# A written order of 2718 commands: the first nine feed-forward pieces, their weight loads and casts stand earlier, and the first 1902 commands and the masks are another fit

## The chip, the cores and the metric

The kernel runs on one core of one Trainium2 chip. A core has TensorE (PE: matrix products, with its weight loads shown apart as PEld), VectorE (DVE), ScalarE (ACT), GpSimd (POOL) and SyncE (SP, which here issues nearly all DMAs). Each engine works through its own queue in the order in which the program was written and waits at an instruction until its operands are there. Products land in PSUM, everything else lives in SBUF.

The metric is the device time of one execution in microseconds, and the median of several. The profile describes one execution more closely; its span runs from the first to the last instruction.

## The reference

Two stages. First an attention with 8 batches, 8 heads, 576 positions and 64 dimensions a head, in which only scores within `tau` = 0.02 of the row's maximum count:

```python
scores = scale * np.matmul(q, k.transpose(0, 1, 3, 2))
thresh = np.max(scores, axis=-1, keepdims=True) - tau
scores = np.where(scores >= thresh, scores, -1000000000.0)
scores = scores - np.max(scores, axis=-1, keepdims=True)
attn = np.exp(scores)
attn = attn / (np.sum(attn, axis=-1, keepdims=True) + 1e-09)
return np.matmul(attn, v).astype(np.float32)
```

Its output, with the heads side by side, is x of 4608 x 512, and a feed-forward stage with three first matrices of 512 x 768 follows:

```python
h = np.maximum(np.maximum(x @ w1, x @ w2), x @ w3)
return (h @ w_out).astype(np.float32)
```

Inputs and output are float32.

## The kernel before

**Tiles.** The eight heads of a batch are handled as two quads of four heads, so there are 16 quads, numbered `g`. A quad's queries are cut into nine chunks; a chunk has 128 rows, two halves `r`, and one half tile is 128 x 576 scores. There are 16 x 9 x 2 = 288 half tiles. The first and the last batch (`SPLIT`) are worked in two parts: part 1 has chunks 0, 1, 5 and 6 of both quads (columns 0 to 255 of x), part 2 the other five (320 columns). So 16 half tiles come before the products of part 1 of batch 0, and 20 more before those of part 2.

**The order written out by hand.** All that comes after a short beginning (`beginning()`: the first transposes and two score tiles) is one text, `ORDER`, of 2718 commands; a command is one letter, and the letters S, T, O, F and D are followed by the number of the PSUM slot (0 to 3, two banks each) in which the result is put. `issue(what, where)` carries them out one after the other. Each letter takes the next item of its own list, so the text says when something is issued and not which. Every engine wrapper (`_Ordered`, line 92 holds its call, which is why all instructions of the profile bear L92) ties each instruction to the one before it on the same engine: the written order is the order in every queue. Here commands are counted from 0. The letters, by engine:

- TensorE: `S` the scores of a half tile (`sc`, two or four fp32 products); `T` the transposition of a quad's q or k (`tp`); `O` and `N` the products of probabilities and v (`o`); `D` spreads the first two quads' row scales (`d`); `F` the first eight matmuls of a feed-forward piece, `B` the other eight (both `ph`, or `po` where the piece is one of the output product).
- VectorE: `m` a half tile's maximum (a pass over 576 columns that accumulates); `k` the numerators of a half tile whose bit in `MASKED` is 1; `r`, `R` reciprocals; `c` copies k out of PSUM; `w` copies a product; `v` the maximum of a feed-forward product with what there is (`hm`, at the third matrix into `hT`).
- ScalarE: `e` the first pass over a half tile (an exponential with a 1 bit, else a leaky ramp `Prelu`); `n` the second pass, an exponential, for a half tile whose bit is 0; `a` copies q out of PSUM; `b`, `x`, `u` copies out of PSUM; `h` the copy of the first matrix's feed-forward product (`hm`).
- GpSimd: `p` scales a half tile's numerators to bf16 (`P`, from quad 2 on); `q` makes the copy of q with the halves of the partitions swapped (`qs`); `y` casts v; `z` casts one staged weight block of 128 x 1024 to bf16.
- SP: `l` one load of a quad's q, k or v; `g` one weight load of 512 KB into a `stage` buffer, of which there are two; `t` the DMA transposition of a chunk's `P` into `ptq`; `o` a store of 128 rows of the output.

**The masks.** A half tile's numerators are 0 for scores under the threshold. Two ways give the same values: with the bit at 1, `m` on VectorE writes -score to SBUF, `e` on ScalarE is the exponential and `k` on VectorE compares and multiplies; with the bit at 0, `m` keeps only the maximum, `e` is the ramp and `n` on ScalarE the exponential. `MASKED` holds 288 bits, one for each half tile in the order of the steps, and so shares the work between VectorE and ScalarE.

**Feed-forward pieces.** Nine pieces make a part's hidden rows in batch 0: three blocks of two times 128 hidden columns, times three matrices. Each has 16 matmuls of 64 rows by 256 columns (320 in part 2, 288 in later batches), an `h` or `v` step for it, and needs the block of weights that the `z` of the same number has cast, from the `g` of the same number. The first nine `g` and `z` are those of w1, w2, w3, the last three those of w_out. Part 1's pieces also need the four products `O` of part 1, which stand at commands 154 to 200 in this kernel, with their copies `w` until 207.

The lines that bear on it:

```python
elif what == "F":
    p = next(todo["F"])
    p.first(where)
    if p.second:
        pending.append(p)
elif what == "B":
    p = pending.pop(0)
    p.second()
    line[p.kind].extend(p.done)
elif what in "gz":
    next(loads if what == "g" else casts)()
```

Of the kernel before, what the change touches and what calls it, by code (L numbers as in the profile page):

```python
# [21 lines left out]
FLAT = 2.0 ** -100  # L22

MASKED = """
001011001000011010101101101000010111100001101000010100001010000100001000
001010100111100001001001000100110000011100010011001010001010010000111000
110010100101010010011100000001001011000110100110111001000100001110000101
001010001101110001100001000100100100001100001101010110110101000111111111
"""

# [8 lines left out]
PLACE = (0, 1, 4, 5, 6, 2, 3, 7, 8)  # L39

ORDER = """
mS2S3lmS1meenemelllgkllT0S2aqmlmeS3lmgT1lllT0eqckT2ancS0mtqS1qmennktyS3eteS2mznmS1eeS0mnlS3eS2S1mmS3netmegke
S2mS0mmyeS3znnRytyltleeS1nmkkeS0mmeeS2mS1enS0T3kmmktgltlemS1D2aS0eT3blekmmteS2D0O1ckmlO3bNwRwS0mneeD1knS3beT
2nD1tllabS0mS2ketnO1lRktmetmO3qNqtwqwzenT2nS0S1zncS3qymmS2mmeeS1S3D0S2mkmtD1elbeemneS0kmbkT3S1kegmatS2qS3neT
0memknneS2O1O3cNtS0remkwtqerT2pnaRmpS1D0gekrS2bmtlwneS0S3D1mmpplleblppzO2eO1mrqpNnekpS0wwS2nnmzF3S1S0emrmrmk
glBepqpF1pF2ethgzBevT3nBF0S1nncBvhS3S2pmrmgF0ekeT1BatnmrF3vS1BS0peF2rmpypS1lpBnvmezF3nhzBS2mpenekqvS1F0F3mtm
BqerkrBpgvepptT2cS1T0hnamttS3mnrS2tF0myBeS1ppeS2yvnplF3rS0nmemteeBlF1meqptS2pvT3BcmnF0tlS3znkphgglBemS1rvmS2
O3npemO0rknrNeewpF1xpS2qpS0ltntmF3lmneeBBS2S0rvhmF1tntpzleS3mBpF0S2empztvenrpBmpvS1mnS3S2enF0emrpS3pktS1pnme
rmmepBekuS2mkunenrS1S3pF0T2pmmtaBeueukpS1rpqeklmeS2tO3mprO0ekNS1lltlwlS2xmF3nF0BmepT1kBehrcF2nT3T1BvcppS0tlq
aqnllvF3qlmS1mrBprF2S0nekheBnmpvtF3S1BF2eS0mvtprmBypnpS1ehpytpS3mtoS2oeelmtmS0F3lF1meBkevryBT2yenF0vapT3cBT2  # L50
S1lS3naqhpF2qS0rkmBpmmrF3npeS1vempteneBvF2S0ktpmltrllBF3S1lnhnmBqrvpneelS0S2mpmO1ekreO3NT0xS2wcmS3mnpqpnF1F0
pBekpBvS2ertlS3F1htmtltmS0pBnemepynrF3eS2vS0mmrT1atppqeBS2pnpF1vF3meultkS0klT1enormkT2BaS2peS0ortcmnmuurS1pe
T2qpF3cS2mpenenpS0kmetrBmltS1S2puymlueeqpS0pylomO3mO1knNerekxwS0pmS2F3S1npnqmBF2elS0kmtBerkheF3pS1nmeypvBtrm
noF2leS0vpBS3rrmnpmpphS1ppF0etmS2emllBeF1nF3BtevkrpS0BvS2nS1hmmtleS3lmmetF2tkF0eBpleT1BvrvanT3nF2cS1BnmF0S3B
rhkF2mpeT1vnrBpprveaS0S3nmT1S2pqpncmpS0meeeqmeS1tO3pqmtotlloeO2ltqNF0S1klwBxrpkppS3mrhmF2S0epBmF3nenS1pvBF0m
F2nleBBtottvkS3hF0keF1rurvpmT2BeapkppyrpvS1S3mnS2S0pnemF1mtS2emkS3rpBenepltS0memkmrutpuS3neS2emF1rmpqkynpS3p
qeBemS0uuS3O2kmemekO1NeS0rwT3xoF1olppnT2mnT0BcS3aS2rncqhF0qtF1pBtemmpBkevrF3eS2vlmpnBptnlS0S1S2hermmempS3F0y
pmF1BBelrteoevnF2T3F0akkqvBBS3nhkymF1pqpnF2verBBS0rvtpmhnS3S1F2mrmlpBpeS0evlmS3eF1pnS2BmnleF3mtllvrlttS0eppp
tyBmS1ehF2lepT3BmltnS0lnltcS1rkvO3O2tmNpmeprT1nnexrapkwS0pqF2qyemT1T3cpBF0S1anepkBS3hvF2S0mreBF1mekmrnvF3qBe
S2vS0unpS3tS1omlrmeppqptlmmnF2pktT0BpecS1eekryuT3uaS0mnS2lomtmrtleF3enpS1kpS2qppnemmS0BmkerppeueqS1S0mnurO2k  # L60
mO1NkwxT0S3eeS1cmpmF2F0kkeBBhF3eF2pvrBS1nnBvpttS0hmemS3mrppF1rpS2BeenmeF0S3vBF1nkvmS2mlnBS0otolhF3llterlmF1k
BlpypvpBtvteeprS2F0rT3BpS1nnrmpmaS3mtpheS0S2emnF3eT1T0amecBS2ttoS0evyymmS1ppeO3mpqneO2NenqxF0kktF1wBT3lolrlk
lBpS2vphS0cmnF1mtlteS3nqrtBmrpF0vrpqpF2lekBeBpnhF1S3vmT0tlpBS2lS3avmpF0tF1mBrnelekS2evutppmrS3qppS1nS0nmF2mr
mS1peekenpS3BemmeS0rkS1emuS3tlT0ueT2mcknrannpepF1S0mS2qppBmtotlmlttkrrpeueS0qqmS2lO3ueemoeO0opptpkklNwS1lS2x
F3mS0BnemehF1kT2mrcnpBS0F3rvS2BltlpnmF1nepmeveS0pkmBS3httnF2eF1mBrBekF0nS3vrBprvpypppS2nmhemeS1S0F2pF3mmBeBr
T1eS0kvnapS2vF1nS3mnBrmmreS2F0pheS1meeBqpnS3mvmeypS1tpS2etlO0qO3mNpmT2neytF1xtlkkrtnweS3ppT0cramBF2S0Bnehvpp
meS1rF3qqmT2BF0ncveT2ktnBF3vS1mrnarBhppS0lF2T3qppeBmcS0S1ovmF3mneT2naepBvS0S2enF3mkmrkqpqueenF1nS3tmS0T2cpqB
eupurrS2mmottoS3pS0mttneelotpmS1O2mkkO0rNwrpeexpneF3nkpS0S2S1mBemS0euuppmF1erkS2tltlBptmrF3S0lhtpmeyppBeS1mv
O0O2NenmxpS3S1kF0mxemrS2kBF1enF3vBermF0tBhpyppyektBvS1pmF2F3vBkS1BF0nmehS2vrBmtpO3eotpnevO1NkF0S2krmnrpxpxBh
F3S1eBF0mS2F1BnvpmBrS3vS2S0ehemmF1kppmnF3rBvkBF2F0BF1ehBtkvevoF2pptkttO3O0NuprBwS2xS0vmmpeS3ekF1S2pmF0oeBmrB  # L70
okettF3peuokoruoF2uhF1pkkF3hvvruF2pF1F3hppF0pvvF2F1vvF3F0F2hvtovhtF1F3F0F2htvF1voF3O0uvO2NvF1xwF3hF2F0vF3vhF
2F0F3hvF2vvF0F3F2vF0hF3hovF2vF0F3vhF2vvF0vBuuF3BuouoF2uooo
"""


# [731 lines left out]
```

## Time and profile before

| | |
|---|---|
| median of 3 runs | 441.56 us (440.37 to 443.75) |
| the profiled execution | 439.98 us |
| its span | 438.2 us |
| TensorE busy | 420.6 us |
| VectorE busy | 398.2 us |
| ScalarE busy | 387.0 us |
| GpSimd busy | 288.5 us |
| TensorE's granted clock, mean | 1.00 |
| DMA | 87.45 MB, 200 GB/s |

Rows of the profile name an instruction by line, engine, operation and by what it writes and reads (`z<-sc,nm` writes z from sc and nm), then give its shape, the count, the summed busy time and the mean duration in ns of one, and after the second bar the engine's idle time just before them with what ended it. The rows of slices are the span in 40 equal parts of 11 us, each digit the busy share in tenths. Matmuls overlap, so the busy time of TensorE is the time in which at least one was under way, and the ends of matmuls are modelled.

### The profile page before, as it was taken

The numbers are of one execution on the slowest core, as the hardware profiler recorded it, in microseconds if no ns is written. First come the engines' busy times: TensorE is split into PE (matmuls) and PEld (weight loads), VectorE is DVE, ScalarE is ACT, GpSimd is POOL, SyncE is SP. The second block draws the span as 40 slices with busy tenths as digits, with TensorE's granted clock in tenths as the row PEclk, the third lists the DMA queues.
The fourth block names the chain that finished last, engine by engine and source line by source line (L and its number), as shares of the span: only waits on it lengthen the run. The fifth ranks groups of instructions, "written<-read, shape, count | busy, mean of one in ns | idle before, by whom it ended". The sixth has DMA issues, their size and how long they took to land.

```text
span 438.2 us, 14262 instructions
## 1 busy us (share of the span) xinstructions
PE 420.6 (96%) x5313; PEld 306.9 (70%) x5313; DVE 398.2 (91%) x1105; ACT 387.0 (88%) x784; POOL 288.5 (66%) x370
## 2 busy tenths in 40 slices
PE   7679889999999999999999999999999999999995
PEld 5446458776787767867787767877677776777762
DVE  3999999989999999999999999999999999999641
ACT  5999999999999999988999999989999999875422
POOL 3704288978688697596867885678759677554500
PEclk9999999999999999999999999999999999999999
DMA  7999999999999999999899998979989997485602
GB/s 252 302 241 206 221 229 261 237 244 193 211 192 225 229 200 193 205 174 256 185 203 216 222 190 206 212 201 219 201 220 186 246 150 154 110 160 128 177 14 109
DMA packets 212773, 87.45 MB, mean 200 GB/s; under 512 B 185824, under 2 KB 199648, under 8 KB 212704
## 3 DMA queue, kind: packets, MB, share of 16 engines
q1 hardware_dynamic: 212000, 85.69, 92.4%
q8 instruction: 42, 0.69, 0.7%
q10 hardware_dynamic: 704, 0.85, 0.6%
q14 instruction: 27, 0.22, 0.2%
HBM read 34.60 MB, written 9.44 MB: 101 GB/s over the span
## 4 chain that ended last, share of the span: by engine, by line
PE 81%; ACT 9%; DMA 3%; issue 2%; DVE 2%; POOL 2%; SPq 0%; POOLq 0%; DVEq 0%
PE ph L92 30%; PE sc L92 27%; PE po L92 11%; PE o L92 9%; ACT z L92 5%; PE tp L92 3%; DMA ptq<-P 3%; ACT P L92 2%; POOL P L92 1%; DVE z L92 1%; PE warm L92 1%; DVE unused L92 1%; ACT qt L92 1%; DMA out_dram<-ob 1%; PE d L92 0%
## 5 line engine op out<-in xcount | busy, mean ns | idle before, releaser
L92 POOL TENSOR_SCALAR P<-z,rs 128x576 bf16<-128x576 f32 x252 | 206.8, 833 | 78.9 <-DVE rs L92 27.4
L92 PE MATMUL sc<-kt,qt 64*128 64x256 f32 (+2 forms) x640 | 177.1, 421 | 2.7 <-DVE z L92 1.3
L92 PE MATMUL sc<-kt,qs 64*128 64x320 f32 (+2 forms) x640 | 175.5, 410 | 4.0 <-ACT z L92 1.6
L92 PE MATMUL ph<-xt,w 64*128 64x288 bf16 (+4 forms) x2160 | 170.5, 283 | 0.4 <-ACT z L92 0.2
L92 PEld LDWEIGHTS <-w 64*128 64x128 bf16 (+1 forms) x2160 | 124.4, 94 | 33.6 <-issue 6.3
L92 DVE TENSOR_SCALAR_CACHE_REDUCE unused<-sc 128x576 bf16<-128x576 f32 x170 | 124.8, 749 | 4.0 <-PE sc L92 3.2
L92 ACT ACTIVATE z<-sc,nm 128x576 f32<-128x576 f32 x170 | 122.7, 740 | 3.4 <-DVE unused L92 1.6
L92 PEld LDWEIGHTS sc<-kt,qs 64*128 64x128 f32 (+1 forms) x640 | 91.0, 175 | 19.7 <-ACT z L92 6.3
L92 ACT ACTIVATE z<-z 128x576 f32<-128x576 f32 x151 | 102.3, 682 | 0.2
L92 PEld LDWEIGHTS sc<-kt,qt 64*128 64x128 f32 (+1 forms) x640 | 90.4, 175 | 16.3 <-DVE z L92 4.3
L92 ACT ACTIVATE z<-z,nm 128x576 f32<-128x576 f32 x118 | 89.5, 773 | 4.8 <-DVE z L92 4.6
L92 DVE TENSOR_SCALAR_CACHE_REDUCE z<-sc 128x576 f32<-128x576 f32 x118 | 87.5, 751 | 5.6 <-PE sc L92 3.1
L92 DVE SCALAR_TENSOR_TENSOR z<-z 128x576 f32<-128x576 f32 x101 | 80.1, 802 | 0.1
L92 POOL COPY qs<-qt 64x640 f32<-64x640 f32 (+3 forms) x68 | 47.8, 702 | 42.3 <-ACT qt L92 27.7
L92 PE MATMUL po<-wo,hT 64*128 64x512 bf16 (+1 forms) x480 | 53.6, 357 | 0.1
L92 ACT ACTIVATE hm<-ph 128x576 bf16<-128x576 f32 (+4 forms) x54 | 32.1, 594 | 19.9 <-PE ph L92 19.5
L92 DVE TENSOR_TENSOR hm<-ph,hm 128x576 bf16<-128x576 f32 (+4 forms) x54 | 36.9, 684 | 8.5 <-PE ph L92 8.4
L92 PEld LDWEIGHTS <-hT 64*128 64x128 bf16 (+1 forms) x480 | 26.3, 97 | 20.0 <-issue 3.9
L92 DVE TENSOR_TENSOR hT<-ph,hm 128x576 bf16<-128x576 f32 (+4 forms) x54 | 37.1, 688 | 2.4 <-PE ph L92 0.5
L92 PE MATMUL o<-ptq,vb 128*64 128x64 bf16 (+2 forms) x576 | 36.5, 275 | 0.8 <-DMA ptq<-P 0.8
L92 PEld LDWEIGHTS <-vb 128*64 128x64 bf16 x576 | 23.3, 111 | 15.7 <-issue 5.1
L92 ACT ACTIVATION_READ_ACCUMULATOR z<-z 128x1 f32 x151 | 30.0, 199 | 0.0
(40 smaller groups left out, 297.3 us busy)
## 6 DMA issues: line engine op xcount, KB each, us to landing
vm<-in_v_dram SPq DMA_DIRECT2D x32, 256.0 KB, 4.7
out_dram<-ob SPq DMA_DIRECT2D x31, 256.0 KB, 3.2
qm<-in_q_dram SPq DMA_DIRECT2D x15, 512.0 KB, 4.8
km<-in_k_dram SPq DMA_DIRECT2D x15, 512.0 KB, 5.5
stage<-in_moe_w_dram SPq DMA_DIRECT2D x9, 512.0 KB, 5.8
ptq<-P SPq DMA_TRANSPOSE x144, 4.2
stage<-in_moe_w_out_dram SPq DMA_DIRECT2D x3, 512.0 KB, 5.5
qm<-in_q_dram SPq DMA_DIRECT2D x16, 64.0 KB, 3.2
```

What stands on the lines that cost most here:

```text
L92: ins = fn(*a, **kw)
```

## The change

Both texts are replaced, no function and no constant beside them. Every letter occurs as often in the new order as in the old but for `n` and `k`: 118 one bits become 120, so two `n` become `k`. Thirty bits differ, 20 of them in batches 0 and 1, ten in batches 3 to 5.

In the order, the last 816 commands have the same letters and differ in the slots' numbers alone (2 for 1, 3 for 2, 0 for 3, 1 for 0). The commands before them, 1902, are in another order. The largest moves are those of the first nine feed-forward pieces and of what they need:

| command | before, at | after, at |
|---|---|---|
| `F` 1 to 9 | 343, 360, 362, 374, 389, 400, 407, 422, 437 | 214, 239, 254, 273, 300, 304, 316, 333, 385 |
| `F` 10 to 12 | 438, 472, 487 | 434, 467, 485 |
| `g` 1 to 12 | 16, 31, 86, 132, 254, 296, 353, 366, 388, 450, 522, 523 | 22, 30, 91, 111, 219, 238, 266, 295, 314, 419, 495, 519 |
| `z` 1 to 12 | 64, 97, 208, 215, 322, 342, 367, 421, 425, 517, 579, 591 | 51, 61, 141, 187, 235, 270, 313, 327, 371, 517, 562, 588 |
| `O` 1 to 8 | 154, 159, 191, 200, 272, 273, 323, 325 | 155, 163, 195, 204, 287, 293, 360, 363 |
| `h` 1 to 6 | 365, 381, 424, 460, 521, 572 | 231, 280, 328, 447, 513, 581 |

The masks in full, and of the order the first seven lines and the last two that differ:

```diff
--- before.py
+++ after.py
@@ -22,9 +22,9 @@
 FLAT = 2.0 ** -100
 
 MASKED = """
-001011001000011010101101101000010111100001101000010100001010000100001000
-001010100111100001001001000100110000011100010011001010001010010000111000
-110010100101010010011100000001001011000110100110111001000100001110000101
+001010001101110000110100100110001110010001101010010100011010000100011000
+001010100111100001001001000100110000011100010011001010001010010000111001
+010010110100010010011100000001001011010110101001101001000100001110000101
 001010001101110001100001000100100100001100001101010110110101000111111111
 """
 
@@ -39,37 +39,37 @@
 PLACE = (0, 1, 4, 5, 6, 2, 3, 7, 8)
 
 ORDER = """
-mS2S3lmS1meenemelllgkllT0S2aqmlmeS3lmgT1lllT0eqckT2ancS0mtqS1qmennktyS3eteS2mznmS1eeS0mnlS3eS2S1mmS3netmegke
-S2mS0mmyeS3znnRytyltleeS1nmkkeS0mmeeS2mS1enS0T3kmmktgltlemS1D2aS0eT3blekmmteS2D0O1ckmlO3bNwRwS0mneeD1knS3beT
-2nD1tllabS0mS2ketnO1lRktmetmO3qNqtwqwzenT2nS0S1zncS3qymmS2mmeeS1S3D0S2mkmtD1elbeemneS0kmbkT3S1kegmatS2qS3neT
-0memknneS2O1O3cNtS0remkwtqerT2pnaRmpS1D0gekrS2bmtlwneS0S3D1mmpplleblppzO2eO1mrqpNnekpS0wwS2nnmzF3S1S0emrmrmk
-glBepqpF1pF2ethgzBevT3nBF0S1nncBvhS3S2pmrmgF0ekeT1BatnmrF3vS1BS0peF2rmpypS1lpBnvmezF3nhzBS2mpenekqvS1F0F3mtm
-BqerkrBpgvepptT2cS1T0hnamttS3mnrS2tF0myBeS1ppeS2yvnplF3rS0nmemteeBlF1meqptS2pvT3BcmnF0tlS3znkphgglBemS1rvmS2
-O3npemO0rknrNeewpF1xpS2qpS0ltntmF3lmneeBBS2S0rvhmF1tntpzleS3mBpF0S2empztvenrpBmpvS1mnS3S2enF0emrpS3pktS1pnme
 ...
-okettF3peuokoruoF2uhF1pkkF3hvvruF2pF1F3hppF0pvvF2F1vvF3F0F2hvtovhtF1F3F0F2htvF1voF3O0uvO2NvF1xwF3hF2F0vF3vhF
-2F0F3hvF2vvF0F3F2vF0hF3hovF2vF0F3vhF2vvF0vBuuF3BuouoF2uooo
+lS2mS3mlemleS1neT0S2lmeamkmgllS1ekqlgT3T0qnalllncT0emS3cmlqqS2zenyyymS0ttzS1tS2eS3nemmnS0emlS2eememtekmS1eS3
+kmgnltemS0S2eS1nklnmlktmS3gnS2eemS1RkmeT0metlmS2eleS3S1nkmmT3eazyS2emlD0ecmtbD3S1O0tkekmnbO2NRwS3wS1D0ennmqm
+tebeS2D3bkS0T1ztmeaqkqO3nqtmneynO2NkwS1wS3nmS0F2S1mT3mgeBRmceD0klS3khebezS2tgF0S1mneBmlkmteD2vbF3S2T0kmBeS1n
+aengvmezqS0F3mS2BS0mehrT1tS2neO3mecnnO1pgNttmF2qpkF0wwtrrkBT3zgyF1epaBnvvS3BlzhrS2mlF0RemkS1lnBlS2D3pvqD0pel
+mrmppbklO3blO0teNqwpS1zweS2mS3npS0mmmrnF1BevS3T1emckS2emteS0npreptlnpT1S3kpmneptgarS2nmmeeS0pteS1mF3S0rekBmm
+pnlpthlelS2kT3trktpS1epqpcmrF0nT3mtnpqpaBeS3S2evS0mF1yS3mnetmeegrBpF2mvT0crBeS1F3knpnhympzlgnenS0mlBqpeS1vmS
+2O0O3erprmkNF1ekS2xwS3mmrnF0nqBpBepzplttvreS2ttpS3lptF1mmhnS0mBepzpeF3netrvnS2pmBS1pS0vnmtF2mS3S0rekepnepS1m
 ...
+okettF0peuokoruoF3uhF2pkkF0hvvruF3pF2F0hppF1pvvF3F2vvF0F1F3hvtovhtF2F0F1F3htvF2voF0O1uvO3NvF2xwF0hF3F1vF0vhF
+3F1F0hvF3vvF1F0F3vF1hF0hovF3vF1F0vhF3vvF1vBuuF0BuouoF3uooo
```

More of the change, by code (lines that the diff above doesn't have):

```diff
@@ L47 @@
-BqerkrBpgvepptT2cS1T0hnamttS3mnrS2tF0myBeS1ppeS2yvnplF3rS0nmemteeBlF1meqptS2pvT3BcmnF0tlS3znkphgglBemS1rvmS2
-O3npemO0rknrNeewpF1xpS2qpS0ltntmF3lmneeBBS2S0rvhmF1tntpzleS3mBpF0S2empztvenrpBmpvS1mnS3S2enF0emrpS3pktS1pnme
-rmmepBekuS2mkunenrS1S3pF0T2pmmtaBeueukpS1rpqeklmeS2tO3mprO0ekNS1lltlwlS2xmF3nF0BmepT1kBehrcF2nT3T1BvcppS0tlq
-aqnllvF3qlmS1mrBprF2S0nekheBnmpvtF3S1BF2eS0mvtprmBypnpS1ehpytpS3mtoS2oeelmtmS0F3lF1meBkevryBT2yenF0vapT3cBT2
-S1lS3naqhpF2qS0rkmBpmmrF3npeS1vempteneBvF2S0ktpmltrllBF3S1lnhnmBqrvpneelS0S2mpmO1ekreO3NT0xS2wcmS3mnpqpnF1F0
@@ L52 @@
[L52 to L70, printed above, removed]
-okettF3peuokoruoF2uhF1pkkF3hvvruF2pF1F3hppF0pvvF2F1vvF3F0F2hvtovhtF1F3F0F2htvF1voF3O0uvO2NvF1xwF3hF2F0vF3vhF
@@ new lines @@
+mrmppbklO3blO0teNqwpS1zweS2mS3npS0mmmrnF1BevS3T1emckS2emteS0npreptlnpT1S3kpmneptgarS2nmmeeS0pteS1mF3S0rekBmm
+pnlpthlelS2kT3trktpS1epqpcmrF0nT3mtnpqpaBeS3S2evS0mF1yS3mnetmeegrBpF2mvT0crBeS1F3knpnhympzlgnenS0mlBqpeS1vmS
+2O0O3erprmkNF1ekS2xwS3mmrnF0nqBpBepzplttvreS2ttpS3lptF1mmhnS0mBepzpeF3netrvnS2pmBS1pS0vnmtF2mS3S0rekepnepS1m
+emreptBltkuS3upmmS0rF1lltpS2lnneekmmT3rBS0aS2kkueuepO3O1qlpqpmrpmekNeS0wmpxS2mF3F1rknBepeT0hplBcF2T3tnvT0Bta
+S1ncF3qS0vBnmF2qyS1BemhrrkemF3S0nBvpF2pmepnpS1vBrmS0yeS3hemS2S1yylmlpF3plmmtleF0BlBkeetevrnF2T1T3vltoaBhT0tp
@@ new lines @@
+S1rapnknqS2F0cmmeS3BeF2pqS1mrBvpF0emS3ntppleBvrF2topytnS1kmmBS3hnS0O1vmlepnO2NeqmrkreeT3qS0xtptwcnnF2S1mmkF3
+BlpveprBeS0lmS1ppF2hnmeS3rmpyBS1pnS0plvF3ntlT2mmeBaS1olevF2F3kmeueS2enrkrT0qT1tpBmakcepS1muS2urS0mopT3F1ntyp
+pcS3leqkrenS2pppmmrneBS3memlupS0mS2uetetO1O3mnekrknpNwxS2S0S1pmpF3BemnF0mlqetS2kqreBtltpheF3knS1mBvprmF0vppe
+S2nrBS3epnS1mrmmF2phS0BF1mveeF3kBS2epvenrBlnhnltS0mS1elolpmtltS3F0F2etypmmBkevyBpeT1rT3vF0ancS1BF2otnhmrS3BF
+0kmtlplevrT1pppqpBtnltS2aS1oeT3rvmcS0nneS2meS3mqO1mmO0pppqeNeqkkreF2xwS3BS0pmpnhS1metnemF3F2lBkrlS1vBF0mrpve
@@ new lines @@
+npF3eBBhnkpvF2S1T0F3aurkBS0mltleS3rvS1mppmmlpqS2F0S1mtolnS2pqpteeemBrkneepS3ultuS1pmrmS2F0peepS3ymmkkntemeoB
+nttS1rS2uuO3kppemmrkeO0leNS1xloT2T0npawS3mF1T0rclBcS2enmF0hprqqpmkeF1tpenBS3tttpntvmBoF2eS0vBmrS3S1yppmhS0mF
+2eF3BBemepeF1nkT0vkrBF2vanhS0kBnF3F1mrBvBvppqS2petnS0prlpqrolmlmhnepS3F1mtltolBevleS2S0tmnnetF3pS1BmF0rmlepy
+S2evBS3hmF1enT0pkBmcrppnvS2S3O0O1rmnNenpmeS3kxerwF2T1aT0mnBT3cvaF1S0ppBheqqprkplmS2eF3S1BmkvnF2eF0mkuqppBenl
+S3S0vtrmtS1lmpprmpptF2S3lT0BtmttelteeocS3kekT1ruumS0aS2nmF1mkqrpS0enpeS3BermmkS2euS3pmuenS0qpO1mpyO2qmerekNp
@@ new lines @@
+xT0newS3cS2mleF1mF0BottpllykpBlhrtkF3pevF1BnnS2nvrmBS0mS3lhF2mpS1lotemyepeBpF0S3lvBnenF2tnS1BrkhmvpmtlypS3F0
+F2eermkBBS1eF3vnnT0BrvpprrampypttltthS2S0mmS3emF1T0eS2T3cBpqS0mqS2nevemmyaeS3pmkeO1llktO0NpqpekeF2nxnlT3BF0c
+rS3BwlvppmtrS1mnotoF2hS0enBmrpF1vrpqpF3lekBeBpnhF2S0vmT1tlpBS3lS0avmpF1tF2mBrnelekS3evutppmrS0qppS2nS1nmF3mr
+mS2peekenpS0BemmeS1rkS2emuS0tlT1ueT3mcknrannpepF2S1mS3qppBmtotlmlttkrrpeueS1qqmS3lO0ueemoeO1opptpkklNwS2lS3x
+F0mS1BnemehF2kT3mrcnpBS1F0rvS3BltlpnmF2nepmeveS1pkmBS0httnF3eF2mBrBekF1nS0vrBprvpypppS3nmhemeS2S1F3pF0mmBeBr
@@ new lines @@
+T2eS1kvnapS3vF2nS0mnBrmmreS3F1pheS2meeBqpnS0mvmeypS2tpS3etlO1qO0mNpmT3neytF2xtlkkrtnweS0ppT1cramBF3S1Bnehvpp
+meS2rF0qqmT3BF1ncveT3ktnBF0vS2mrnarBhppS1lF3T0qppeBmcS1S2ovmF0mneT3naepBvS1S3enF0mkmrkqpqueenF2nS0tmS1T3cpqB
+eupurrS3mmottoS0pS1mttneelotpmS2O3mkkO1rNwrpeexpneF0nkpS1S3S2mBemS1euuppmF2erkS3tltlBptmrF0S1lhtpmeyppBeS2mv
+O1O3NenmxpS0S2kF1mxemrS3kBF2enF0vBermF1tBhpyppyektBvS2pmF3F0vBkS2BF1nmehS3vrBmtpO0eotpnevO2NkF1S3krmnrpxpxBh
+F0S2eBF1mS3F2BnvpmBrS0vS3S1ehemmF2kppmnF0rBvkBF3F1BF2ehBtkvevoF3pptkttO0O1NuprBwS3xS1vmmpeS0ekF2S3pmF1oeBmrB
```

## The prediction

> **What bounds the kernel now.** I read the page first, then the same busy times cut at the points where the mix of work changes, then the chain of work that ended last.
>
> ```profile
> span 438.2 us, 14262 instructions
> ...
> PE 420.6 (96%) x5313; PEld 306.9 (70%) x5313; DVE 398.2 (91%) x1105; ACT 387.0 (88%) x784; POOL 288.5 (66%) x370
> ...
> PE   7679889999999999999999999999999999999995
> ...
> DVE  3999999989999999999999999999999999999641
> ACT  5999999999999999988999999989999999875422
> ```
>
> Three engines are nearly full for most of the span. TensorE's row is short of 9 only at the left, VectorE's and ScalarE's only in the first slice and at the right, so in the first sixth the two elementwise engines set the pace, and in the last tenth TensorE works alone. The next view gives busy time by stretch (columns: TensorE, its weight loads, VectorE, ScalarE, GpSimd, each with its count, then clock, DMA share, GB/s).
>
> ```profile
> 0.00:20.00 20.00, 14.61 (x143) 10.87 (x145) 12.74 (x33) 14.53 (x30) 10.81 (x22) 1.00 0.93 278
> 20.00:65.00 45.00, 37.82 (x434) 23.24 (x434) 43.48 (x130) 43.99 (x92) 17.94 (x22) 1.00 1.09 225
> 65.00:376.00 311.00, 310.49 (x4052) 230.51 (x4051) 300.23 (x838) 298.68 (x605) 238.44 (x304) 1.00 1.01 209
> 376.00:438.20 62.20, 57.66 (x694) 42.24 (x688) 41.73 (x109) 29.80 (x60) 21.27 (x24) 1.00 0.45 111
> ```
>
> TensorE idles 5.4 us before 20 us, 45 - 37.82 = 7.2 us from 20 to 65, 0.5 us in the 311 us after that, and 4.5 us at the end, which is the last store. The whole possible gain from a fuller TensorE lies in the second row. But in that same row VectorE idles only 1.5 us and ScalarE 1.0 us. Is the 311 us stretch TensorE at its own pace, or TensorE stretched by waits? Rows of the chain (start, length, what) answer it.
>
> ```profile
> 324.98 0.54 PE sc L92 x4
> 325.52 0.49 PE ph L92 x8
> 326.01 0.43 PE sc L92 x4
> 326.44 2.45 PE ph L92 x40
> ...
> 376.81 3.43 PE ph L92 x56
> ```
>
> Eight `ph` matmuls take 0.49 us alone between two score tiles, 2.45 / 5 = 0.49 in a run, and 3.43 / 7 = 0.49 at 377 us, where VectorE and ScalarE have slack. So TensorE runs at its own rate from 65 us on, and changing from score to feed-forward matmuls costs nothing that can be seen (0.54 + 0.49 or 0.43 + 0.60 a pair). From there every microsecond of TensorE idleness added or removed moves the end by as much.
>
> The Trainium skill, page "Perfetto Trace Analysis", section "Identifying the Most-Contended Engine", speaks against this reading: TensorE's matmul busy share is no good measure, and the busy share of the weight loads should be taken, which is 70% here. The rows above are why I don't follow it; what it would make of the time is the fourth rival.
>
> **The change part by part.** The counts of every command are the same in both orders, the last 816 of 2718 commands differ only in the PSUM slots' names, and no tile size changes. So TensorE's work is the same 420.6 us, and the sum is made of its idle time alone.
>
> *The nine pieces.* The first `F` goes from command 343 to 214 (counted from 0) and the ninth from 437 to 385. From the tenth on the positions are within five commands (438 and 434, 472 and 467, 487 and 485). When do these commands run? GpSimd's casts are marks on the way: those written at commands 208, 322, 342, 367 and 421 start at these times.
>
> ```profile
> 41.55 2.02 POOL L92 CAST w<-stage 128x1024 bf16<-128x1024 f32 x2
> ...
> 61.45 1.03 POOL L92 CAST w<-stage 128x1024 bf16<-128x1024 f32 x1
> ...
> 65.17 1.04 POOL L92 CAST w<-stage 128x1024 bf16<-128x1024 f32 x1
> ...
> 70.64 1.03 POOL L92 CAST w<-stage 128x1024 bf16<-128x1024 f32 x1
> ...
> 75.99 2.02 POOL L92 CAST w<-stage 128x1024 bf16<-128x1024 f32 x2
> ```
>
> That is (75.99 - 41.55) / (421 - 208) = 0.16 us a command, so the first piece moves from about 66 us to about 42.5 us, and the ninth from about 78 to about 70.
>
> ```profile
> 65.89 0.60 PE L92 MATMUL ph<-xt,w 64*128 64x256 bf16 x7
> 66.33 0.43 PE L92 MATMUL sc<-kt,qt 64*128 64x320 f32 x1
> ```
>
> Eight of these 256-column matmuls take 66.33 - 65.89 = 0.44 us, a piece has sixteen, nine pieces are 7.9 us of TensorE. Before 65 us there is 7.2 us of idle time, about half of it after 42.5 us:
>
> ```profile
> 45.00:50.00 5.00, 4.33 (x40) 2.53 (x40) 4.81 (x15) 4.57 (x10) 0.34 (x1) 1.00 1.27 216
> 50.00:55.00 5.00, 3.72 (x42) 2.15 (x44) 4.83 (x15) 5.00 (x13) 1.43 (x2) 1.00 0.94 216
> 55.00:60.00 5.00, 4.24 (x78) 2.69 (x74) 5.00 (x17) 4.88 (x11) 3.85 (x4) 1.00 1.19 220
> 60.00:65.00 5.00, 4.24 (x64) 2.91 (x64) 3.97 (x13) 4.81 (x10) 4.84 (x7) 1.00 1.12 225
> 65.00:70.00 5.00, 5.00 (x72) 3.97 (x71) 4.76 (x15) 4.40 (x10) 3.71 (x6) 1.00 0.99 246
> ```
>
> Between 45 and 65 us TensorE idles 0.67 + 1.28 + 0.76 + 0.76 = 3.5 us. The pieces can take that. But each brings an elementwise step, and those are moved ahead with it.
>
> ```profile
> L92 ACT ACTIVATE hm<-ph 128x576 bf16<-128x576 f32 (+4 forms) x54 | 32.1, 594 | 19.9 <-PE ph L92 19.5
> ...
> L92 DVE TENSOR_TENSOR hm<-ph,hm 128x576 bf16<-128x576 f32 (+4 forms) x54 | 36.9, 684 | 8.5 <-PE ph L92 8.4
> L92 DVE TENSOR_TENSOR hT<-ph,hm 128x576 bf16<-128x576 f32 (+4 forms) x54 | 37.1, 688 | 2.4 <-PE ph L92 0.5
> ```
>
> Three copies and six maxima: 3 x 0.59 = 1.8 us of ScalarE and 6 x 0.69 = 4.1 us of VectorE enter a stretch in which both are full, and push softmax steps back. The text agrees: by command 343 the new order has issued eight more `F` but three fewer `S`, `m` and `e`. By command 485 the two orders are level in `F`, `S`, `m` and `e`. So the pieces are ahead for some 45 us and then ahead no longer; what has been won by then is only what all engines together have won, and VectorE and ScalarE are the cap.
>
> *The cap.* ScalarE can win at most its idle time, 1.0 us (20 to 65); VectorE 1.5 us. Further idle time lies up to 100 us.
>
> ```profile
> 65.00:85.00 20.00, 19.84 (x280) 15.12 (x279) 19.59 (x56) 19.37 (x42) 18.50 (x23) 1.00 1.13 266
> 85.00:90.00 5.00, 4.83 (x61) 3.69 (x59) 3.99 (x10) 5.00 (x12) 4.84 (x8) 1.00 1.15 177
> ```
>
> That adds 0.4 + 1.0 for VectorE and 0.6 for ScalarE, so 2.9 us and 1.6 us.
>
> *The masks.* Thirty bits differ, 118 ones become 120. A one moves a half tile's numerator from ScalarE to VectorE.
>
> ```profile
> L92 ACT ACTIVATE z<-sc,nm 128x576 f32<-128x576 f32 x170 | 122.7, 740 | 3.4 <-DVE unused L92 1.6 <-POOL P L92 0.7
> L92 ACT ACTIVATE z<-z 128x576 f32<-128x576 f32 x151 | 102.3, 682 | 0.2
> ...
> L92 ACT ACTIVATE z<-z,nm 128x576 f32<-128x576 f32 x118 | 89.5, 773 | 4.8 <-DVE z L92 4.6
> ...
> L92 DVE SCALAR_TENSOR_TENSOR z<-z 128x576 f32<-128x576 f32 x101 | 80.1, 802 | 0.1
> ```
>
> ScalarE is relieved of 740 + 682 - 773 = 0.65 us a bit (a read of its accumulator beside it), VectorE charged 0.80 us. Up to command 485 one more numerator goes to VectorE: ScalarE's cap rises to about 2.3 us, VectorE's falls to about 2.1 us, and the lower one holds. Over the whole order two bits move, 1.3 us and 1.6 us, which hide behind TensorE after 65 us (12.3 and 10.8 us of room in the 311 us row); without that cover VectorE's 1.6 us would come in full. Of the cap of 2.1 us (the bounds are 0 and 2.1) I expect half: **-1.0 us**.
>
> *Loads, casts and queues.* The fifth to ninth weight loads are issued 35 to 87 commands earlier, each 512 KB on SP's queue in front of transposes; the twelve casts stay on GpSimd.
>
> ```profile
> stage<-in_moe_w_dram SPq DMA_DIRECT2D x9, 512.0 KB, 5.8
> ptq<-P SPq DMA_TRANSPOSE x144, 4.2
> ```
>
> The fifth load stands at command 219 and its cast at 235: 16 x 0.16 = 2.6 us for a 5.8 us landing, so GpSimd stands still for about 3 us at 45 us; behind it wait the sixth cast and the swaps of quad 3, which no score tile needs before command 385, and GpSimd was idle there (0.34 us busy from 45 to 50). That costs nothing; without this cover it is 3 us. The seventh piece follows its cast by three commands and the eighth by six, and the eighth's load precedes it by 38 commands, 6.2 us, where landing and cast take 5.8 + 1.0. I bound the two waits by 0 and 1.5 us and take 0.3, because TensorE idles 1.5 us between 55 and 65 us anyway. On SP the five issues now stand ahead of transposes that they followed, but the last transpose that batch 0's products need has 53 commands until the product instead of 40, 2 us more room.
>
> *The rest fitted anew.* From command 485 to 1902 the order is reshuffled. TensorE idles 0.5 us there now, so nothing can be won. What can be lost isn't in this trace. Below it is bounded by -0.5; above by the rate of the 20 to 65 us row, 7.2 / 45 = 16%, or some 35 us, which is far off. The nearest row is that of 85 to 90 us, 0.17 of 5, the rate at which an order with the same engines full leaves holes; over 30 us of such places it is 1 us. I take half of that, **+0.5 us**, because the old order does without.
>
> Sum: -1.0 + 0.3 + 0.5 = -0.2 us on the profiled execution's 439.98 us (span 438.2 and 1.8 around it), 439.8 us. That execution lies 1.6 us under the median of 441.56 us; in the median's terms **441.4 us**.
>
> **The rivals.** One per cent, 4.4 us, is about what a measurement of this kernel can tell from no change.
>
> 1. The whole cap is won, the elementwise engines run without a hole, and TensorE leaves the stage two score tiles (0.54 us each) further ahead: -2.1 - 1.0 = -3.1 us, 438.5. For it: VectorE's 1.0 us hole between 60 and 65 us lies ahead of products that have more room now. Against it: nothing in the new order's counts at command 485 is ahead. Chance 0.16, of which 0.05 beyond 1%.
> 2. The change doesn't do what it says: the pieces are written earlier, but five of them wait for weights, TensorE stands in front of the score tiles behind them, VectorE and ScalarE lose what the wait is long. With landings of 7.8 us instead of 5.8, 2 us at the seventh and eighth each, less 1.5 us of cover: +2.5 us on the forecast, 443.9. For it: the DMA share is at 1.27 and 1.19 at 45 to 60 us. Against it: two loads lie between. Chance 0.13, 0.02 beyond 1%.
> 3. The other side: the order after 85 us no longer feeds TensorE. VectorE has only 10.8 us of room in 311 (3.5%), so a tile read late keeps its PSUM slot and the next score tile stands in TensorE's queue with everything behind it. The place is 85 to 300 us. It decides from 4.4 us plus the 1 us won early, 5.4 in 215 us: 2.5%, 0.5 us in each 20. At 3%, 6.5 us of holes less that 1 us give 447.1. For it: none of the three engines has slack to hide a misplaced step, and ten of the changed mask bits, in batches 3 to 5, shift load between VectorE and ScalarE there. Against it: the old order shows 0.5 us in 311, so it can be done. Chance 0.27, 0.25 beyond 1%.
> 4. TensorE isn't the bound after 65 us, VectorE is; then a better order may win VectorE's idle 10.8 us there, 441.6 - 10.8 = 430.8. The equal 0.49 us at 326 and 377 us speak against it. Chance 0.02. This is where the skill's rule on weight loads, named above, would lead.
>
> **How the numbers follow.** The forecast has 0.42. Faster by over 1%: 0.05 + 0.02 = 0.07. Slower: 0.25 + 0.02 = 0.27. Within 1%: 0.66. The range runs from 438.0, just under the first rival, to 446.5, which takes in the second and the lower half of the third; some 0.07 lie below and 0.13 above.
>
> **What would show it.** ScalarE's copies of the feed-forward pieces mark the order in time; the tenth piece's, and that of the last third of batch 0, now start here:
>
> ```profile
> 81.55 0.70 ACT L92 ACTIVATE hm<-ph 128x640 bf16<-128x640 f32 x1
> ...
> 98.67 0.70 ACT L92 ACTIVATE hm<-ph 128x640 bf16<-128x640 f32 x1
> ```
>
> They stand at commands 460 and 572, in the new order at 447 and 581, so I expect the first near 79 us and the second at 98 to 100. The first `ph` matmul comes near 42 us. TensorE's idle time from 20 to 65 us falls to 4 to 5 us, with VectorE and ScalarE at 43.5 to 44.5 us there. From 65 to 376 us TensorE idles under 2 us. I am wrong if the second copy comes before 96 us (then the cap was no cap), if TensorE's holes after 85 us add up to over 4 us (the third rival), if the pieces' matmuls stand in waits for their weights (the second), or if TensorE's summed busy time changes by more than 2 us.

## The result, and the profile after

The changed kernel takes 440.28 us (median of 20 runs) where the kernel before takes 442.31 us (20 runs beside it): a ratio of 0.9952 with a 95% interval from 0.9929 to 0.9976, so it is faster by 1.1 to 3.1 us. The profiled execution took 439.23 us, its span is 437.1.

The page's rows that answer to those of before, then the busy time by the same stretches:

```profile
span 437.1 us, 14271 instructions
...
PE 420.2 (96%) x5313; PEld 305.8 (70%) x5313; DVE 398.9 (91%) x1109; ACT 386.1 (88%) x780; POOL 289.8 (66%) x370
...
PE   7769998899999999999999999999999999999995
...
DVE  3999999999999999999999999999999999999641
ACT  5999989999999999999999999989999999875422
```

```profile
0.00:20.00 20.00, 15.38 (x149) 11.55 (x149) 12.72 (x33) 14.62 (x31) 11.27 (x23) 1.00 0.96 282
20.00:65.00 45.00, 40.31 (x505) 26.99 (x504) 44.41 (x129) 43.46 (x91) 19.47 (x23) 1.00 1.15 243
65.00:376.00 311.00, 307.96 (x3993) 225.93 (x3991) 301.08 (x846) 299.18 (x602) 237.80 (x303) 1.00 1.04 206
376.00:437.10 61.10, 56.59 (x679) 41.35 (x675) 40.66 (x104) 28.84 (x58) 21.21 (x24) 1.00 0.43 113
```

TensorE's work is the same, 420.2 us for 420.6. From 20 to 65 us it idles 4.7 us instead of 7.2, but from 65 to 376 us 3.0 instead of 0.5. Finer stretches of the same view show where the idle time went (columns: TensorE, its weight loads, VectorE, ScalarE, GpSimd, then clock, DMA share, GB/s):

```profile
50.00:55.00 5.00, 5.00 (x70) 3.55 (x68) 5.00 (x15) 4.86 (x11) 2.30 (x2) 1.00 1.12 352
55.00:60.00 5.00, 5.00 (x102) 4.05 (x102) 4.87 (x15) 5.00 (x12) 4.11 (x5) 1.00 1.20 244
60.00:65.00 5.00, 5.00 (x74) 3.55 (x70) 4.77 (x14) 3.89 (x9) 4.84 (x7) 1.00 1.25 184
65.00:70.00 5.00, 4.93 (x82) 4.03 (x80) 4.53 (x14) 4.54 (x10) 4.84 (x7) 1.00 1.14 276
70.00:75.00 5.00, 3.77 (x42) 2.15 (x38) 5.00 (x17) 5.00 (x12) 2.62 (x4) 1.00 1.14 159
75.00:80.00 5.00, 4.15 (x36) 2.78 (x36) 5.00 (x17) 5.00 (x11) 4.63 (x6) 1.00 1.06 262
80.00:85.00 5.00, 4.44 (x58) 2.64 (x60) 4.95 (x15) 5.00 (x12) 3.86 (x5) 1.00 1.29 267
```

From 50 to 65 us TensorE has no hole any more. From 70 to 85 us it has 1.23 + 0.85 + 0.56 = 2.6 us of holes where the kernel before had next to none, and there VectorE and ScalarE are at 4.95 to 5.00 of 5: by the order they are working off the softmax steps that the pieces pushed back. The stretch from 65 to 100 us before, then after:

```profile
65.00:100.00 35.00, 34.67 (x461) 26.14 (x460) 32.89 (x92) 34.19 (x74) 30.37 (x39) 1.00 1.11 241
65.00:100.00 35.00, 32.29 (x404) 22.31 (x401) 34.14 (x99) 33.97 (x70) 30.43 (x39) 1.00 1.12 231
```

From 20 to 100 us TensorE thus idles 7.5 us before (7.2 + 0.3) and 7.4 now (4.7 + 2.7): the hole was moved, not filled. Over the whole span its idle time falls by 0.7 us, 17.6 to 16.9, and by windows that lies before 20 us, where it idles 4.6 us for 5.4. VectorE is busy 2.2 us more from 20 to 100 us, but it also has two numerators more in that part of the order, 0.80 us each, so the profile alone doesn't say how much of this is won.

ScalarE's copies of the feed-forward pieces (first, fourth and sixth; rows of the timeline) mark the way:

```profile
46.16 0.60 ACT L92 ACTIVATE hm<-ph 128x512 bf16<-128x512 f32 x1
...
79.49 0.70 ACT L92 ACTIVATE hm<-ph 128x640 bf16<-128x640 f32 x1
...
97.54 0.70 ACT L92 ACTIVATE hm<-ph 128x640 bf16<-128x640 f32 x1
```

The sixth comes 1.1 us earlier than before, though nine commands (1.4 us) more stand ahead of it. In a second profile of the same kernel (after_again, below) it comes at 99.22, so one execution alone can't carry a gain of this size; the timed runs have to.

### The profile page after: what moved, and what is told of

It reads as the page before. It is cut to its first block, busy times and chain, and to the rows that moved or that the text cites. A ratio compares the mean times of both kernels' runs of the same rounds, so it can differ in the third digit from the quotient of the medians.

```text
span 437.1 us, 14271 instructions
## 1 busy us (share of the span) xinstructions
PE 420.2 (96%) x5313; PEld 305.8 (70%) x5313; DVE 398.9 (91%) x1109; ACT 386.1 (88%) x780; POOL 289.8 (66%) x370
## 4 chain that ended last, share of the span: by engine, by line
PE 84%; ACT 6%; DVE 5%; issue 2%; DMA 2%; ACTq 0%; DVEq 0%
PE ph L92 32%; PE sc L92 28%; PE po L92 11%; PE o L92 8%; ACT z L92 4%; PE tp L92 4%; DVE z L92 2%; DVE unused L92 1%; ACT P L92 1%; DMA km<-in_k_dram 1%; DMA qm<-in_q_dram 1%; DVE P L92 1%; ACT qt L92 1%; PE d L92 0%; DVE kt L92 0%
## 5 line engine op out<-in xcount | busy, mean ns | idle before, releaser
L92 PE MATMUL sc<-kt,qt 64*128 64x256 f32 (+2 forms) x640 | 179.5, 422 | 4.2 <-DVE z L92 2.0
L92 PE MATMUL sc<-kt,qs 64*128 64x320 f32 (+2 forms) x640 | 177.4, 411 | 3.0 <-ACT z L92 1.3
L92 ACT ACTIVATE z<-z 128x576 f32<-128x576 f32 x148 | 100.4, 682 | 0.3
L92 ACT ACTIVATE z<-z,nm 128x576 f32<-128x576 f32 x120 | 91.3, 774 | 4.7 <-DVE z L92 4.4
L92 DVE TENSOR_SCALAR_CACHE_REDUCE z<-sc 128x576 f32<-128x576 f32 x120 | 89.3, 752 | 5.1 <-PE sc L92 3.7
L92 DVE SCALAR_TENSOR_TENSOR z<-z 128x576 f32<-128x576 f32 x104 | 81.0, 789 | 0.1
```

The costliest lines, as they stand in the source:

```text
L92: ins = fn(*a, **kw)
```

## Experiments

Twelve runs, one of them the changed kernel once more, each timed in five rounds beside the kernel before. The changed kernel came out at 0.9952 at first and at 0.9940 when it ran again (after_again); "on the changed kernel" below is against the latter for the three runs that were timed with it (pe_mid24, act_early, masks_old), and against the mean of the two, 0.9946, for the rest, with some 1.3 us of uncertainty either way. My theory: up to 65 us VectorE and ScalarE set the pace, after it TensorE, and the change can win what idle time the two have there. The rivals: the refit of the later commands wins; TensorE's total work counts everywhere; VectorE is the bound also after 65 us.

### Front and rear apart

At command 618 (about 102 us) both orders have issued the same set of commands (but for two `n` that are `k` in the new one), so they can be cut and joined there.

```diff
 front_new:
-commands 0 to 617 of the old order, mask bits 0 to 99 old
+commands 0 to 617 of the new order, mask bits 0 to 99 new
 commands 618 to 2717 of the old order (PSUM slots 2 and 3 exchanged), mask bits from 100 on old
```

> The first 618 commands (to about 102 us) in the new order with their mask bits, the other 2100 in the old order with theirs; at command 618 both orders have issued exactly the same work. Theory (the gain is won ahead of 85 us, where TensorE's idle time is filled): the whole difference of -2.0 us, so 440.3 where the kernel before has 442.3, between -1.0 and -3.0. Rival (the refit after command 618 is what wins): 0 within 0.7 us.

Measured: 442.14 us for 444.63, ratio 0.9943 (0.9920 to 0.9965). That is as much as the whole change measured.

```diff
 rear_new:
 commands 0 to 617 of the old order, mask bits 0 to 99 old
-commands 618 to 2717 of the old order, mask bits from 100 on old
+commands 618 to 2717 of the new order, mask bits from 100 on new
```

> The other half: the first 618 commands and their mask bits old, the rest and its mask bits new. Theory: TensorE had 0.5 us of idle time there, so 0 within 0.7 us. Rival (the refit wins): -1.3 to -2.7 us.

Measured: 442.90 us for 444.63, ratio 0.9973 (0.9945 to 1.0000): -1.2 us, in between the two expectations, and the interval ends at no change. The stretch from 100 to 376 us of both profiles gives no reason for a gain: TensorE idles 0.2 us before and 0.3 us after (the rows of before, then of after).

```profile
100.00:376.00 276.00, 275.82 (x3595) 204.37 (x3593) 267.34 (x747) 264.49 (x533) 208.07 (x266) 1.00 1.00 204
100.00:376.00 276.00, 275.66 (x3595) 203.63 (x3591) 266.94 (x748) 265.21 (x533) 207.37 (x265) 1.00 1.03 202
```

The front is enough for the result. That the rear adds nothing isn't shown: the two medians are 0.8 us apart, the two profiled executions happen to be equally long (spans of 439.6 and 439.8 us), and the sum of both halves, 0.84%, was not seen in the whole.

### One part alone, one part undone

```diff
 pieces_alone (old order and masks):
-F B h v of pieces 1 to 9, g 5 to 9, z 3 to 9 at their old places
+the same commands after as many of the other commands as in the new order
+18 elementwise commands drawn forward where no PSUM slot would be free
```

> The old order and masks, but the first nine feed-forward pieces with their copies and maxima, the weight loads 5 to 9 and the casts 3 to 9 stand where the new order has them; 18 elementwise commands are drawn forward where no PSUM slot would be free. Nothing else is fitted. If filling TensorE's idle time is what counts, -1 to -2 us, as the whole change. If VectorE and ScalarE are the cap and the move must be fitted into their queues, the gain is lost: 0 to +4 us.

Measured: 454.52 us for 444.63, ratio 1.0215 (1.0177 to 1.0252): +9.9 us. The move alone wins nothing; it costs about five times what the whole change wins. Its stretches from 20 to 65 and from 65 to 100 us:

```profile
20.00:65.00 45.00, 35.75 (x418) 23.67 (x416) 40.14 (x116) 38.53 (x81) 14.98 (x17) 1.00 1.09 229
65.00:100.00 35.00, 28.70 (x306) 20.15 (x303) 24.77 (x71) 26.29 (x55) 23.96 (x31) 0.85 0.93 189
```

All engines lose: VectorE 4.9 us idle instead of 1.5, then 10.2 of 35, where the kernel before idles 2.1. A row of GpSimd's timeline, and one of TensorE's, say what it waits for:

```profile
55.52 2.46 POOL L92 CAST w<-stage 128x1024 bf16<-128x1024 f32 x2 [11.90 <-DMA stage<-in_moe_w_dram]
```

```profile
57.54 0.50 PE L92 MATMUL sc<-kt,qt 64*128 64x320 f32 x1 [2.34 <-DVE hT L92]
```

The fifth cast and the sixth come at 55.5 us, GpSimd has stood 11.9 us for the weights (in the changed kernel the fifth cast is done by 49 us), and a score tile stands 2.3 us until a piece's maximum frees its slot, with VectorE and ScalarE starved behind it. This is my second rival, at a price four times as high as I gave it; it didn't happen in the change. That this is because loads, transposes and score tiles around the pieces were placed with them is likely, but no run separates it.

```diff
 pieces_undone (new order and masks):
-F B h v of pieces 1 to 9, g 5 to 9, z 3 to 9 at their new places
+the same commands after as many of the other commands as in the old order
+10 elementwise commands drawn forward where no PSUM slot would be free
```

> The new order and masks, but those same commands put back to where the old order has them; 10 elementwise commands are drawn forward where no PSUM slot would be free. If the pieces' place is the cause, +1 to +4 us on the changed kernel, at or above the kernel before. If the refit of the rest of the first 485 commands is the cause (masks, loads, score tiles), no more than +1 us on the changed kernel.

Measured: 448.20 us for 444.63, ratio 1.0086 (1.0055 to 1.0117): +6 us on the changed kernel, over the range that I gave. The sixth copy of ScalarE comes at 106.85 us there. About 1 us of the 6 goes with TensorE's granted clock (see the last section): the three executions with a mean clock of 0.999 or 1.00 took 447.2 us, the five at 0.988 to 0.996 took 448.1 to 449.3.

```diff
 masks_old (new order):
-the 288 new mask bits
+the 288 old mask bits; each half tile's numerators keep their place in the text
+8 elementwise commands drawn forward where no PSUM slot would be free
```

> The new order with the old mask bits: the 30 half tiles go back to the engine that they had, each numerator at the place in the text that the new order gives it; 8 elementwise commands are drawn forward where no PSUM slot would be free. If the masks belong to the gain (the order was fitted with them), +1 to +4 us on the changed kernel beside it; if they don't matter, 0 within 1 us.

Measured: 458.12 us beside 441.80 of the changed kernel, +16.3 us, a ratio to before of 1.0306 (1.0278 to 1.0333). Thirty half tiles whose numerators sit in the other engine's queue cost more than anything else that I tried:

```profile
20.00:65.00 45.00, 35.95 (x366) 23.18 (x364) 38.86 (x109) 37.53 (x77) 11.93 (x14) 0.92 1.03 234
65.00:100.00 35.00, 31.12 (x406) 21.79 (x400) 30.00 (x88) 31.41 (x66) 26.71 (x34) 0.95 0.92 194
```

VectorE and ScalarE idle 6.1 and 7.5 us from 20 to 65 us, with the same sum of work but for two numerators. Not all of the loss is early: from 100 to 376 us TensorE idles 5.2 us, where it idles 0.3 in the changed kernel. Neither these bits nor the old ones are better in themselves; what this shows is the price of an order that doesn't fit its masks.

The three runs together: no part was seen to win by itself. A part put out of step with the others costs 6 to 16 us, the repairs (the commands drawn forward, some PSUM slots renumbered) included, and in step they win 2. Which part of the fitted front wins them is not separated; the new masks in the old order, and the rest of the new front without pieces and masks, were not run.

### What an engine's microsecond costs, early and late

The changed kernel, with one instruction issued twice for some half tiles. Results and waits stay the same; only one engine gets more work.

```diff
+TWICE = tuple(range(20, 36, 2))        # early; mid: range(100, 148, 6), 24: range(100, 196, 4)
-        for x in (1, 0):
+        for x in (1, 0) * (2 if 2 * number[2 * L["b"] + L["qd"], idx] + r in TWICE else 1):
```

> The changed kernel, but the score matmuls of 8 half tiles (every second one of those between 20 and 40 us) are issued twice into the same PSUM slot: 8 x 0.54 = 4.3 us more work for TensorE and nothing else; the result is the same. Theory (there VectorE and ScalarE set the pace and TensorE idles 4.3 us in 20): 0 to +1.5 us on the changed kernel, a ratio to the kernel before of 0.995 to 0.999. Rival (TensorE's total is what counts everywhere): +4.3 us, 1.005.

Measured: 442.07 us for 444.98, ratio 0.9944 (0.9916 to 0.9971): nothing, -0.1 us on the changed kernel. TensorE's added work there is free within the measurement; the page has 424.2 us of busy TensorE, 4.0 more than the changed kernel's first profile and 2.2 more than its second.

> The same 4.3 us of doubled score matmuls, for 8 half tiles (every sixth) between about 130 and 190 us. Theory (TensorE runs at its own rate there without a hole): +4 to +4.5 us on the changed kernel, a ratio of 1.005. Rival (VectorE is the bound there, TensorE's busy share misleads): 0 to +2 us, up to 1.000.

Measured: 444.07 us for 444.98, ratio 0.9988 (0.9960 to 1.0015): +1.9 us, between the expectations and less than I gave. So I tripled the dose:

> The changed kernel with the score matmuls of 24 half tiles doubled (every fourth between about 130 and 260 us), three times the dose of the run with 8: 24 x 0.54 = 13 us more TensorE work. Theory (TensorE at its own rate after 65 us): +12 to +13.5 us on the changed kernel beside it, 2.7 to 3.0%. Rival (TensorE is only partly the bound there, as the +1.6 us for 4.3 us of the first dose suggest): +3 to +8 us.

Measured: 452.96 us beside 441.80, +11.2 us. The page of this run and of the changed kernel beside it (the run called after_again) give the dose that was really there:

```profile
PE 433.7 (96%) x5421; PEld 321.5 (71%) x5421; DVE 401.9 (89%) x1109; ACT 388.3 (86%) x780; POOL 287.0 (64%) x370
```

```profile
PE 422.0 (96%) x5313; PEld 306.5 (70%) x5313; DVE 399.4 (91%) x1109; ACT 386.5 (88%) x780; POOL 288.3 (66%) x370
```

By these two, TensorE is busy 11.7 us more, 0.49 us a doubled tile and not 0.54, and the time rises by 11.2 (some 1.6 either way). Its idle time over the whole span is the same, 16.8 us of 450.5 and 16.7 of 438.7: TensorE's late work costs its full length. The dose itself is less sure, since the changed kernel's first profile has 420.2 us busy with the same work, 1.8 less. In the run with 8 tiles the page has 424.9 us, 2.9 or 4.7 more, beside 1.9 us of time: it agrees with the smaller dose within the measurement, not with the larger.

> The changed kernel once more, as the mark that the runs beside it are measured against: a ratio to the kernel before of 0.993 to 0.998.

Measured: 441.80 us for 444.05, ratio 0.9940 (0.9916 to 0.9964).

The same with VectorE's pass for the maximum (both forms of it) and with ScalarE's first pass:

```diff
+TWICE = tuple(range(20, 36, 2))        # dve_early; dve_mid: range(100, 148, 6)
+            for _ in range(2 if 2 * number[c["g"], c["idx"]] + r in TWICE else 1):
-            vector.tensor_scalar(out=unused, in0=c[r], scalar1=tau, scalar2=None,
-                                 op0=OP.subtract, op1=OP.max, accum_out=nm)
+                vector.tensor_scalar(out=unused, in0=c[r], scalar1=tau, scalar2=None,
+                                     op0=OP.subtract, op1=OP.max, accum_out=nm)
```

> The changed kernel, but VectorE's pass for the maximum is done twice for the 8 half tiles of the early run: 8 x 0.68 = 5.4 us more of VectorE between 20 and 40 us; the result is the same. Theory (VectorE is the cap there): +4 to +6 us on the changed kernel, a ratio of 1.004 to 1.009. Rival (TensorE's total counts and its 16.9 us of idle time take the delay): 0 to +2 us.

Measured: 447.03 us for 444.98, ratio 1.0064 (1.0039 to 1.0090): +5.3 us for 5.4 us of work.

> The same doubled pass for the 8 half tiles of the middle run: 5.4 us of VectorE spread over some 60 us. Theory (TensorE bound, VectorE with 3% of room, 2 us in those 60): +1 to +3.5 us on the changed kernel, a ratio of 0.998 to 1.003. Rival (VectorE is the bound after 65 us): +5.4 us, 1.0075.

Measured: 445.62 us for 444.98, ratio 1.0027 (1.0001 to 1.0052): +3.6 us, at the upper end. From 130 to 195 us, the changed kernel and then this run:

```profile
130.00:195.00 65.00, 64.74 (x860) 47.10 (x855) 63.94 (x176) 63.06 (x130) 50.08 (x65) 1.00 1.05 217
```

```profile
130.00:195.00 65.00, 62.21 (x810) 44.84 (x806) 63.71 (x179) 59.82 (x123) 44.77 (x59) 1.00 0.99 206
```

VectorE idles 1.1 us of those 65 in the changed kernel, not the 2 that the mean over 311 us promised, and 1.3 in this run: the profile shows no room that the added work used, and TensorE gets the holes (2.8 us for 0.3). The timed runs leave 1.8 us of the 5.4 free, with 1.3 of uncertainty.

```diff
+TWICE = (16, 17, 20, 22, 23, 25, 26, 29)
-            scalar.activation(out=zn, in_=c[r], func=AF.Prelu, bias=c["bias", r], scale=-1.0, alpha=FLAT)
+            for _ in range(2 if 2 * number[c["g"], c["idx"]] + r in TWICE else 1):
+                scalar.activation(out=zn, in_=c[r], func=AF.Prelu, bias=c["bias", r], scale=-1.0, alpha=FLAT)
```

> The changed kernel, but ScalarE's first pass is done twice for 8 half tiles with a 0 bit between 16 and 40 us: 8 x 0.63 = 5.0 us more of ScalarE; the result is the same. Theory (ScalarE is as full as VectorE there): +4 to +5.5 us on the changed kernel beside it. Rival (VectorE alone is the cap): 0 to +2 us.

Measured: 446.36 us beside 441.80, +4.6 us for 5.0 us of work; ratio to before 1.0040 (1.0017 to 1.0064). Its stretch from 20 to 65 us, after that of dve_early:

```profile
20.00:65.00 45.00, 35.55 (x378) 22.39 (x375) 43.86 (x124) 38.17 (x77) 11.07 (x14) 0.92 1.07 230
```

```profile
20.00:65.00 45.00, 37.24 (x392) 23.60 (x392) 39.48 (x110) 43.90 (x87) 11.81 (x15) 0.92 1.05 226
```

Whichever of the two gets the work stays full (43.9 of 45). The other falls back by 5.3 and 4.9 us against the changed kernel, TensorE by 4.8 and 3.1. The 0.92 in both rows is a granted clock that was half for 6.8 us. It isn't what the time went on: VectorE idles 1.1 us of its 45 in the first run, 0.5 more than in the changed kernel, and ScalarE 1.1 in the second, 0.4 less, so nearly all of the loss is the added work.

The theory stands: early, a microsecond of VectorE or ScalarE costs a microsecond and one of TensorE nothing; late, one of TensorE costs all of it, and VectorE is so close behind that of 5.4 us of its work 3.6 come through.

## Why the prediction was right or wrong

The range held and the likeliest class, within 1%, came true; the forecast of 441.4 us lies 1.1 us over the measured 440.28. Part of that closeness is luck: the forecast difference was -0.2 us, next to none, and the measured one is -2.0 (1.1 to 3.1), but the three runs from which the forecast started have a median 0.75 us under that of the twenty beside the changed kernel.

- **What bounds the kernel: right.** The doubled instructions show both halves of it, up to 65 us and after. The fourth rival (VectorE alone the bound after 65 us) is out: with 24 doubled score tiles TensorE's 11.7 us came through as 11.2. The Trainium skill ("Perfetto Trace Analysis", "Identifying the Most-Contended Engine") judges TensorE's headroom by MFU (the matmul work done as a share of the peak) and the busy share of the weight loads, 70% here; after 65 us these runs show no headroom.
- **The cap of 2.1 us, half of it won: mis-sized.** The step that failed is the -1.0 us of my sum. The front half alone, with no other change, measured 0.9943, -2.5 us (1.6 to 3.6): that takes in the whole cap, and the first rival's -3.1 us too. With the whole cap, the 0.4 us of waits below and nothing for the refit the sum is -2.1 + 0.4 = -1.7 us, inside the measured 1.1 to 3.1. The profile shows VectorE's side in part: 43.48 us busy from 20 to 65 before, 44.41 now, 0.9 us of its 1.5 us of idle time used. That the gain is this idle time is the reading that fits; no run shows it by itself.
- **TensorE's holes after 65 us under 2 us: wrong.** They are 3.0 us. I let the pieces fill 45 to 65 us and took the stretch after it as it was. But pieces that are early in one stretch are missing in the next, and there the elementwise engines are in arrears: 2.6 us of holes from 70 to 85 us. My own sentence that the orders are level again at command 485 says as much; I didn't carry it into TensorE's row. From 20 to 65 us TensorE idles 4.7 us, as forecast (4 to 5).
- **Casts and queues: right in kind and size.** GpSimd's standstill for the fifth weight load, which I put at about 3 us at 45 us and covered, is here, and the pieces waited 0.4 us in all for casts, for the 0.3 us of the sum (the rows of the timeline, then of the waits from 20 to 100 us):

```profile
47.61 1.41 POOL L92 CAST w<-stage 128x1024 bf16<-128x1024 f32 x1 [3.20 <-DMA stage<-in_moe_w_dram]
51.43 1.58 POOL L92 CAST w<-stage 128x1024 bf16<-128x1024 f32 x1 [2.41 <-DMA stage<-in_moe_w_dram]
```

```profile
POOL w L92 <- DMA stage<-in_moe_w_dram: 15.8, 4, 8.7
...
PEld L92 <- POOL w L92: 0.4, 2, 0.3
```

  That the third cast would stand for 8.7 us at 20 to 29 us I had not seen; GpSimd next had to wait for ScalarE anyway.
- **The refit after 85 us, +0.5 us: nothing of it came.** TensorE idles 0.3 us from 100 to 376 us, and the rear half by itself is not slower (0.9945 to 1.0000). The third rival, with its 0.27, did not happen.
- **The marks in time:** first `ph` matmul at 44.2 us for 42 to 43, the fourth copy at 79.5 for 79, the sixth at 97.5 for 98 to 100.

## What to carry to other kernels

Idle time of one engine is worth something only where the others have room: find which engine is full in that very stretch, add up its idle time, and that is the most that filling the hole can win. Work moved into a hole leaves a hole where it was taken from, so look at the stretch behind as well. In an order that is written out for five queues, a part that is moved must be fitted together with its neighbours, loads and engine assignments; the parts of this change couldn't be priced by taking them out one by one, since each cost three to eight times the gain when it was out of step.

## What the runs showed that I had not expected

TensorE's granted clock fell to half for a while in the profiles of six of the twelve runs, with no pause of TensorE over 1.8 us in the 9 us before. One of them is the run with VectorE's doubled passes between 130 and 190 us, whose first 100 us have the changed kernel's commands unaltered. Stretches of 1 us:

```profile
23.00:24.00 1.00, 0.43 (x4) 0.30 (x4) 1.00 (x3) 1.00 (x3) 0.00 (x0) 1.00 0.45 72
24.00:25.00 1.00, 0.51 (x6) 0.14 (x4) 1.00 (x5) 1.00 (x4) 0.00 (x0) 1.00 1.02 389
25.00:26.00 1.00, 1.00 (x10) 0.39 (x12) 1.00 (x3) 1.00 (x4) 0.00 (x0) 0.87 1.24 276
26.00:27.00 1.00, 0.86 (x9) 0.01 (x1) 1.00 (x5) 1.00 (x5) 0.00 (x0) 0.50 1.22 288
...
31.00:32.00 1.00, 1.00 (x7) 0.90 (x5) 1.00 (x3) 1.00 (x3) 0.77 (x2) 0.50 1.13 300
32.00:33.00 1.00, 0.92 (x6) 0.38 (x2) 1.00 (x5) 0.66 (x1) 0.00 (x0) 0.71 1.28 289
```

By the shares 0.87 and 0.71 the clock was half from 25.7 to 32.6 us, 6.8 us. The longest pause of TensorE in the 9 us before was 0.85 us:

```profile
23.57 0.48 PE L93 MATMUL sc<-kt,qt 64*128 64x256 f32 x1 [0.85 <-ACT z L93]
```

The seven such spells in the first 100 us of the six profiles last 3.4, 6.8 or 10.2 us each (by the same shares, in stretches of 0.1 us): one, two or three times 3.41 us.

The changed kernel's own profile has the same pauses to a hundredth of a microsecond (0.85 us before 23.55) and a clock of 1.00 throughout. So the same commands can keep the clock or lose it. TensorE is thinly filled ahead of this spell (0.43 and 0.51 from 23 to 25 us), but as thinly in the profile that kept its clock (0.45 and 0.52), so what takes the clock down is not shown. The Trainium skill, "TensorE: Matmul & The Clock Gate", section "Why this matters for your kernels", warns of idle gaps over about 3 us; here the clock fell with no gap over 0.85 us in the 9 us before, and the measurement decides. It cost this run nothing that can be seen up to 65 us (VectorE 44.50 us busy from 20 to 65 as in the changed kernel, 44.41). In the two worst experiments the clock fell as well (0.85 of full from 65 to 100 us with the pieces alone, 0.92 from 20 to 65 us with the old masks); how much of their loss that is was not separated.

The kernel before loses its clock too: of its 23 executions beside front_new, the eight with a mean clock of 0.997 or more took 443.7 us on average, the eight at 0.991 or less 445.2. So a rival is that the change only keeps the clock up. The executions with a mean clock of 0.997 or more speak against it: front_new's five average 441.7 us beside those 443.7, the same 2 us, with some 1.4 us of uncertainty.
